# Three edits to a fused attention and two-layer MoE kernel: where tile 2, 3 and 20's softmax and the weight sums run

## The chip, the cores and the metric

One core of a Trainium2 chip runs the whole program. The metric is the device time of one execution in microseconds (us). The kernel before was timed in three runs: 1226.52, 1226.36 and 1223.59 us, median 1226.36 us. The profiled execution took 1226.5 us by the same clock. Its trace covers a span of 1224.7 us, so 1.8 us lie outside the span.

The engines are TensorE (PE; its weight loads are PEld), VectorE (DVE), ScalarE (ACT), GpSimd (POOL) and the sync engine (SP), which issues nearly all DMAs. Each engine works through its own instruction list in order.

## The reference

```
# attention in chunks of 64 rows, 8 heads of 64, 8 batches of 576 rows
scores = q_c @ k_c.T / 8;  attn = exp(scores - max) / (sum + 1e-9);  out = attn @ v_c
x = out as (4608 tokens, 512)
# first layer, w_in 512x2048, w_out 2048x512
h = x @ w_in;  g = h * clip(h + 3, 0, 6) / 6;  x = g @ w_out
# second layer, w_in2 512x1024, w_out2 1024x512
h = x @ w_in2;  solu = h * softmax(h)
y = (solu - mean) / sqrt(var + 1e-6) * g_ln @ w_out2
```

All inputs are float32. Products are done in three passes of a high and a low part: x = hi + lo, x @ w = hi @ w_hi + hi @ w_lo + lo @ w_hi.

## The kernel before, in words

**Tiles and blocks.** The 4608 tokens are 36 tiles of 128 tokens for the attention and 9 blocks of 512 tokens (four tiles) for the first layer. d_ff = 2048 is cut into 16 chunks of 128. The order of all work is the order of the program text (`manual_schedule`): no planner moves anything, an instruction waits only for its data, for its buffer and for the ones before it on its engine.

**The start (L563 to L628).** Tiles 0 to 3 go through attention before any product of the first layer can run. `attn_scores` (L403) takes row maxima on DVE (L398), subtracts them on DVE (L406) and does one exp over the tile on ACT (L410). `attn_norm` (L431) sums rows on DVE (L437), adds 1e-9 (L438), takes the reciprocal (L439) and multiplies (L440), for these four tiles on POOL. `attn_transpose` (L444) turns a tile on PE (L448) and copies it out of PSUM on ACT (L450). `attn_pv` (L465) multiplies by v, casts the high part on ACT (L472); `attn_lo` (L489) subtracts the low part on DVE (L491). Between these, weights are brought from their stored form to hi and lo parts: ACT rescales (L154), DVE takes signs (L163) and words (L171), ACT casts hi (L352), DVE subtracts lo (L358). The second form of softmax, `attn_scores_act` and `attn_exp_act` (L413, L418), does eight exps per tile on ACT, one for each head, straight from PSUM, each with the negative maximum as bias and the row sum as a second output; it is used from tile 4 on. PSUM holds `att` (one buffer), `acc0`, `acc1` and two `hp` buffers.

**Block 0 (L1264).** For each chunk f, PE does hp(f) (12 products, L498), then ACT a Relu (L504), DVE the gate (L513), ACT the cast g_hi (L520), DVE g_lo (L523), and PE adds the chunk before into acc (12 products, L537, `o_next`). DVE and ACT also convert the weights of later chunks in this block. Every fourth chunk has an attention slot for a tile of block 1.

**Blocks 1 and 2 (L1300, F = 0 to 31).** Here the gate writes into PSUM (L508). In every odd F up to 25 there is an attention slot (`att_slot`, L926): scores of one tile and the product with v of another, both into `att`, so the scores of a tile wait until the exps of the one before have read `att`. The exps of a tile run half in one F and half in the next (STEPS, L1287), then comes its norm and 16 transposes of 32x128 on DVE (L460). The weight sums of the seven-product scheme, for j = 0 to 7: `sums_of(j)` at the end of F = 3j on POOL (L993 to L998), then at F = 3j + 1 two casts hi on ACT (L1005) and two subtractions lo on POOL (L1011) with four DMA stores (L1013), through the four `xo` buffers that also take the finished block (L548, L550) on its way to `x2d`.

**The first pair (L1116).** Blocks 3 to 8 go in three pairs, with seven products in place of eight (`mul7`, L1035), for j = 0 to 7: A11, S2, S1, `o_next`, S3, A12, gate and split, `o_next`, `att_slot`, A22, S4. `prep(0)` (L1068) makes the seven operands in eleven steps during F = 21 to 31. Tile 20 (NA) has its scores at F = 25, its softmax in the first form and its norm and transposes (`soft`, `attn_transpose_dve`) inside j = 0 of the pair.

Of the kernel before, what the change touches and what calls it, by code (L numbers as in the profile page):

```python
# [21 lines left out]
def tile_kernel(  # L22
# [394 lines left out]

    def attn_exp_act(u, hs):  # L418
        sc, mx = exps[u]
        if u not in sums:  # L420
            p_t[u] = att_tile(ap2, "p")
            sums[u] = asp.tile([P, H], F32, tag="sm", name="sm")
        for h in hs:
            a, c = h // 2, h % 2
            m = c * NHP + a
            nc.scalar.activation(
                out=p_t[u][:, h], in_=sc[:, c, a], func=AF.Exp, scale=0.125,
                bias=mx[:, m : m + 1], accum_out=sums[u][:, h : h + 1],
            )

    def attn_norm(u, eng=nc.vector):  # L431
        pt = p_t[u]
        if u in sums:
            sm = sums.pop(u)
        else:
            sm = asp.tile([P, H], F32, tag="sm", name="sm")
            nc.vector.tensor_reduce(out=sm, in_=pt, axis=AX.X, op=ALU.add)  # L437
        nc.vector.tensor_scalar_add(out=sm, in0=sm, scalar1=1e-9)  # L438
        nc.vector.reciprocal(out=sm, in_=sm)  # L439
        eng.tensor_mul(  # L440
            out=pt, in0=pt, in1=sm[:, :, None].to_broadcast([P, H, D])
        )

    def attn_transpose(u, pb=None):  # L444
        pt = p_t.pop(u).rearrange("p (a c) k -> p a (c k)", a=NHP)
# [3 lines left out]
        pb = pts[:, u % 2] if pb is None else pb  # L449
        nc.scalar.copy(out=pb, in_=tp.rearrange("p a (e q) -> p (a e) q", e=2))  # L450

# [128 lines left out]
    fetch("o", 1)  # L580
    fetch("i", 3)
    attn_norm(0, nc.gpsimd)
    attn_scores(2, scores(2, att_psum()), qps[0][:, 1])
    attn_norm(1, nc.gpsimd)
    attn_scores(3, scores(3, acc_psum(0)), qps[1][:, 1])
    attn_transpose(0)
    rescale("i", 0)
    attn_norm(2, nc.gpsimd)
    attn_transpose(1)
    attn_pv(0, acc_psum(1), *xs, lo=False)  # L590
    load_v(4)
    fetch("o", 2)
    fetch("i", 4)
    convert(("i", 0))
    attn_norm(3, nc.gpsimd)
    attn_pv(1, att_psum(), *xs, lo=False)
    attn_transpose(2, kbs[0][:, 1])
    load_v(5)
# [4 lines left out]
    attn_lo()  # L603
    split_w(1, nc.vector)
    attn_pv(2, acc_psum(0), *xs, kbs[0][:, 1], lo=False)
    attn_lo()
    rescale("i", 1)
    attn_transpose(3, kbs[1][:, 1])
    attn_lo()
    attn_pv(3, acc_psum(1), *xs, kbs[1][:, 1], lo=False)  # L610
    rescale("o", 0)
    convert_signs(("i", 1))
    attn_lo()
    attn_scores_act(4, scores(4, att_psum()))
    for f in range(5, NF):
# [7 lines left out]
    convert_signs(("o", 0))  # L623
    split_w_lo(nc.vector)
    convert_words()
    rescale("i", 2)
# [359 lines left out]

    def sums_of(j):

        w, s = ([ap1.tile([P, DM], F32, tag=f"tx{i}", name=f"tx{i}") for i in range(2)], None)
        k = slice(0, 2 * P), slice(2 * P, DM)  # L990
        for i in range(2):
            t = wi[2 * j + i].bitcast(F32)
            nc.gpsimd.tensor_add(out=w[i], in0=t[:, 0], in1=t[:, 1])  # L993
# [6 lines left out]

    def split_sums_hi(j):
        s = summed[j]
        hi, lo = ([work_tile("xo", F32R) for _ in range(2)] for _ in range(2))
        for i in range(2):
            nc.scalar.copy(out=hi[i], in_=s[i])  # L1005
        summed[j] = s, hi, lo

    def split_sums_lo(j):
        s, hi, lo = summed.pop(j)
        for i in range(2):  # L1010
            nc.gpsimd.tensor_sub(out=lo[i], in0=s[i], in1=hi[i].bitcast(F32))  # L1011
            for n, t in enumerate((hi[i], lo[i])):
                nc.sync.dma_start(out=sts[j][:, n, i * DM : (i + 1) * DM], in_=t.bitcast(F32))  # L1013

# [99 lines left out]
    h_t2, second = {}, []  # L1114

    def pair(p, todo):  # L1116
        b1, b2 = FIRST + 2 * p, FIRST + 2 * p + 1
# [5 lines left out]
        for j in range(NJ):  # L1123
# [9 lines left out]
            if hang:  # L1133
                t, f = hang
                g = moe_split(t, nc.gpsimd)
                pend.append((b1, f, g))
            while todo:
                todo.pop(0)()
            if u < NU:
                soft(u)  # L1140
# [5 lines left out]
            nc.vector.tensor_add(out=u2, in0=s1, in1=b)  # L1146
            if u < NU:
                attn_transpose_dve(u, range(4))
# [134 lines left out]

    NA = (FIRST + 2) * UPB
    SLOT_AT = {1 + 2 * n: n for n in range(NA - 2 * UPB + 1)}
    PREP_AT = {21: 1, 22: 1, 25: 1, 26: 2, 27: 1, 28: 2, 29: 1, 30: 1, 31: 1}
    STEPS = {}  # L1287
# [12 lines left out]
    for F in range(2 * NF):  # L1300
# [3 lines left out]
        hp, t = moe_h(f, *xn[b])  # L1304
        moe_gate_there(hp, t)
        for step, u, which in STEPS.get(F, []):
            if step == "turn":
# [3 lines left out]
        if F in SLOT_AT:  # L1311
            u = 2 * UPB + SLOT_AT[F]
            att_slot(u - 1 if u > 2 * UPB else None, u + 1 if u + 1 < NA else NA if u == NA else NU)
        o_next()
        for step, u, which in STEPS.get(F, []):
# [5 lines left out]
        if F % 3 == 0 and F // 3 < NJ:  # L1321
            sums_of(F // 3)
        elif F % 3 == 1 and F // 3 < NJ:
            split_sums_hi(F // 3)
            split_sums_lo(F // 3)
        if F < 8:
# [200 lines left out]
```

## Time and profile before

| what | value |
|---|---|
| median of three runs | 1226.36 us (1223.59 to 1226.52) |
| the profiled execution, its span | 1226.5 us, 1224.7 us |
| busy PE, DVE, ACT, POOL | 1190.7, 952.3, 656.9, 381.8 us |
| chain that ended last, PE's share | 83% |
| PE busy in the first 20 us, in the next 20 us | 20 us window: 10.68, 14.81 us |

Busy time is what an engine spends in instructions; the rest of the span it stands idle. The granted clock of TensorE is a share of its full speed: 1.00 is 2.4 GHz, and at 1.2 GHz it is 0.50; a window with 0.91 holds some of each. In a row of the timeline the first number is the start in us from the start of the span, the second the time covered (for xN, from the start of the first to the end of the last), and in brackets stand the idle time of the engine just before and what ended it.

### The profile page before, as it was taken

How to read it: one execution, taken by the hardware profiler on the slowest of the kernel's cores; microseconds unless marked ns; L12 is line 12 of the kernel's file. 1: busy time of each engine (PE TensorE's matmuls, PEld its weight loads, DVE VectorE, ACT ScalarE, POOL GpSimd, SP SyncE). 2: the span in 40 equal slices, each digit the busy share in tenths (PEclk: the TensorE clock that was granted, in tenths of full speed). 3: DMA queues.
4: the chain of work that ended last, by engine and by line, in shares of the span. 5: the costliest groups of instructions: out<-in, count | busy, mean ns of one | idle time of the engine just before them, and what ended most of it. 6: DMA issues, size and time to landing. Idle time of an engine off the chain costs nothing.

```text
span 1224.7 us, 20699 instructions
## 1 busy us (share of the span) xinstructions
PE 1190.7 (97%) x7268; PEld 970.7 (79%) x7268; DVE 952.3 (78%) x1754; ACT 656.9 (54%) x1353; POOL 381.8 (31%) x466
## 2 busy tenths in 40 slices
PE   6899999999999999999999999999989999999998
PEld 5677788878788888888888888887768888888887
DVE  7999687787677779777778777774997878878774
ACT  4676455453322237322246343363788777877775
POOL 3000243530011110011100112100676767665865
PEclk9999999999999999999999999999999999999999
DMA  9800584441355537355445798794222323232311
GB/s 369 362 26 27 210 304 132 159 152 61 104 198 207 194 108 249 108 189 190 175 138 201 264 335 291 252 377 174 86 68 90 99 71 99 72 97 69 100 54 63
DMA packets 110360, 199.82 MB, mean 163 GB/s; under 512 B 14000, under 2 KB 49072, under 8 KB 107184
## 3 DMA queue, kind: packets, MB, share of 16 engines
q1 hardware_dynamic: 103920, 186.97, 44.1%
q10 hardware_dynamic: 6336, 11.54, 2.5%
q8 instruction: 57, 0.93, 0.3%
q14 instruction: 47, 0.39, 0.1%
HBM read 129.50 MB, written 58.20 MB: 153 GB/s over the span
## 4 chain that ended last, share of the span: by engine, by line
PE 83%; DVE 11%; ACT 2%; issue 1%; DMA 1%; SPq 1%; POOL 1%; DVEq 0%; ACTq 0%; POOLq 0%
PE acc L537 28%; PE po L882 14%; PE hp L1040 14%; PE hp L498 7%; PE att L1040 5%; PE b L684 5%; PE c L684 3%; PE a L684 3%; PE att L386 3%; DVE s L171 2%; DVE g_lo L523 1%; SPq L797 1%; DVE s L163 1%; DVE pbd L460 1%; PE att L684 1%
## 5 line engine op out<-in xcount | busy, mean ns | idle before, releaser
L537 PE MATMUL acc<-g_hi,wo 128*128 128x512 f32 x1152 | 294.9, 393 | 1.4 <-ACT g_hi L520 1.3
L537 PEld LDWEIGHTS acc<-g_hi,wo 128*128 128x128 f32 x1152 | 215.4, 189 | 48.8 <-DVE xo L550 1.9
L523 POOL TENSOR_TENSOR g_lo<-t,g_hi 128x512 fp32r<-128x512 f32 x45 | 65.6, 1457 | 450.8 <-ACT g_hi L520 450.8
L537 PE MATMUL acc<-g_lo,wo 128*128 128x512 f32 x576 | 160.0, 389 | 1.3 <-DVE g_lo L523 1.3
L882 PE MATMUL po<-wi,wo 128*128 128x512 f32 x648 | 152.5, 392 | 1.3 <-ACT ob L891 1.3
L882 PEld LDWEIGHTS po<-wi,wo 128*128 128x128 f32 x648 | 122.6, 189 | 27.5 <-ACT ob L891 1.7
L1040 PE MATMUL hp<-wi,ws 128*128 128x512 f32 x576 | 142.7, 390 | 0.0
L460 DVE STREAM_TRANSPOSE pbd<-p 32x128 f32<-32x128 f32 x448 | 135.5, 303 | 6.7
L537 PEld LDWEIGHTS acc<-g_lo,wo 128*128 128x128 f32 x576 | 108.2, 188 | 24.3 <-DVE g_lo L523 1.7
L1040 PEld LDWEIGHTS hp<-wi,ws 128*128 128x128 f32 x576 | 107.9, 188 | 23.7 <-DVE s L1146 1.2
L665 POOL TENSOR_TENSOR x_lo<-xr,x_hi 128x768 fp32r<-128x768 f32 (+1 forms) x32 | 70.3, 2218 | 135.0 <-DVE xr L651 64.0
L797 ACT COPY wo<-wo 32x256 f32<-32x256 f32 x228 | 92.0, 404 | 17.4 <-DVE wo L779 11.3
L498 PE MATMUL hp<-x_hi,wi 128*128 128x512 f32 x384 | 97.9, 397 | 2.0 <-ACT wi L352 1.9
L520 ACT CAST g_hi<-t 128x512 fp32r<-128x512 f32 x112 | 69.4, 620 | 53.0 <-DVE t L513 36.0
L498 PEld LDWEIGHTS hp<-x_hi,wi 128*128 128x128 f32 x384 | 72.5, 191 | 18.9 <-ACT wi L352 2.7
L1106 ACT ACTIVATE t<-att,three 128x512 f32<-128x512 f32 x24 | 16.5, 688 | 130.4 <-PE att L1040 113.8
L769 DVE SCALAR_TENSOR_TENSOR wo<-wo,r,wo 128x1024 f32<-128x1024 f32 x36 | 77.4, 2151 | 1.3
L1011 POOL TENSOR_TENSOR xo<-tx,xo 128x512 fp32r<-128x512 f32 x16 | 20.8, 1320 | 181.7 <-ACT xo L1005 167.0
L1040 PE MATMUL att<-wi,wa 128*128 128x512 f32 x288 | 73.1, 389 | 0.0
L866 POOL TENSOR_TENSOR wo<-wo,wo 128x1024 fp32r<-128x1024 f32 x26 | 63.4, 2439 | 6.8 <-ACT wo L862 3.3
L1040 PEld LDWEIGHTS att<-wi,wa 128*128 128x128 f32 x288 | 54.1, 188 | 11.3
L504 ACT ACTIVATE t<-hp,three 128x512 f32<-128x512 f32 x48 | 33.1, 691 | 50.4 <-PE hp L498 50.4
(269 smaller groups left out, 2194.6 us busy)
## 6 DMA issues: line engine op xcount, KB each, us to landing
ws<-sts SPq DMA_DIRECT2D x24, 1024.0 KB, 6.7
wa<-stw SPq DMA_DIRECT2D x24, 512.0 KB, 4.0
held<-xo SPq DMA_DIRECT2D x42, 256.0 KB, 2.2
s<-held SPq DMA_DIRECT2D x42, 256.0 KB, 4.4
wo<-wo SPq DMA_DIRECT2D x328, 32.0 KB, 1.8
x2d<-xo SPq DMA_DIRECT2D x36, 256.0 KB, 3.0
out<-ob SPq DMA_DIRECT2D x36, 256.0 KB, 2.2
v<-in_v SPq DMA_DIRECT2D x34, 256.0 KB, 2.7
```

The lines of the kernel that those rows point to most:

```text
L460: nc.vector.transpose(out=pb[o : o + 32, s // 2, s % 2], in_=pv[s * 32 : s * 32 + 32, c, e],)
L498: nc.tensor.matmul(hp, wi[f][:, a, kk * P : (kk + 1) * P], b[:, kk], start=(n == 0), stop=(n == 3 * KD - 1),)
L520: nc.scalar.copy(out=g_hi, in_=t)
L523: eng.tensor_sub(out=g_lo, in0=t, in1=g_hi.bitcast(F32))
L537: nc.tensor.matmul(acc[dc], wo[f][:, w, dc * P : (dc + 1) * P], g[i], start=(at == 0 and n == 0), stop=(at == NF - 1 and n == 2),)
L665: eng.tensor_sub(out=lo[:, f], in0=r, in1=hi[:, f].bitcast(F32))
L684: nc.tensor.matmul(ps, x[:, AT[a], j], w2[w, j][i], start=(start and n == 0), stop=(stop and n == 5), skip_group_check=True,)
L769: nc.vector.scalar_tensor_tensor(out=h, in0=e, scalar=r, in1=h, op0=ALU.mult, op1=ALU.mult, accum_out=mu)
L797: move(out=m[b * 32 : b * 32 + 32, a], in_=tr[a * 32 : a * 32 + 32, b])
L866: eng.tensor_sub(out=lo, in0=m, in1=hi.bitcast(F32))
L882: nc.tensor.matmul(po, a[f], wi[KD * NS + f][:, w], start=(n == 0), stop=(n == 3 * NF2 - 1),)
L1040: nc.tensor.matmul(ps, w[:, i, kk * P : (kk + 1) * P], x[:, kk], start=(start and n == 0), stop=(stop and n == 5), skip_group_check=True,)
```

## The change

Three edits, and two small moves that go with them.

1. Start: tiles 2 and 3 take the second form of softmax, their norm's multiplication moves from POOL to DVE, the copies after the PE transposes of tiles 1 and 3 move from ACT to DVE, and the steps stand in another order. Tile 4's maxima come later. The row sums `sm` get four buffers.
2. Weight sums: `split_sums(j, i)` does one cast, one subtraction and two stores; it runs once per chunk, at F = 3j + 2 and 3j + 3, between the Relu and the cast of g, instead of twice at the end of F = 3j + 1. `sums_of(0)` gets a one-column copy on POOL in front, which reads the low part g[1] of F = 0; for j > 0 there is none (`None if F else g[1]`).
3. Tile 20: its norm runs at the end of F = 27, its transposes at F = 28 and 29, and not inside j = 0 of the first pair. `prep` runs one step later from F = 27 on, its eleventh step (B22) in j = 0 of the pair after the sum u2. The `o_next` of F = 31 is left out there, so two chunks are pending when the pair begins.

```
-    def attn_exp_act(u, hs):
+    def attn_exp_act(u, hs, pt=None):
...
-            sums[u] = asp.tile([P, H], F32, tag="sm", name="sm")
+            sums[u] = asp.tile([P, H], F32, tag="sm", name="sm", bufs=4)
...
-    def attn_transpose(u, pb=None):
+    def attn_transpose(u, pb=None, copy=nc.scalar.copy):
...
-        nc.scalar.copy(out=pb, in_=tp.rearrange("p a (e q) -> p (a e) q", e=2))
+        copy(out=pb, in_=tp.rearrange("p a (e q) -> p (a e) q", e=2))
...
+    attn_scores_act(2, scores(2, att_psum()))
     attn_norm(0, nc.gpsimd)
-    attn_scores(2, scores(2, att_psum()), qps[0][:, 1])
+    attn_scores_act(3, scores(3, acc_psum(0)))
     attn_norm(1, nc.gpsimd)
-    attn_scores(3, scores(3, acc_psum(0)), qps[1][:, 1])
+    attn_exp_act(2, range(H), qps[0][:, 1])
+    rescale("i", 0)
+    attn_exp_act(3, range(H // 2), qps[1][:, 1])
     attn_transpose(0)
-    rescale("i", 0)
-    attn_norm(2, nc.gpsimd)
-    attn_transpose(1)
+    attn_exp_act(3, range(H // 2, H))
+    attn_norm(2)
+    convert_signs(("i", 0))
+    attn_transpose(1, copy=nc.vector.tensor_copy)
+    convert_words()
     attn_pv(0, acc_psum(1), *xs, lo=False)
...
-    convert(("i", 0))
-    attn_norm(3, nc.gpsimd)
+    attn_norm(3)
+    split_w_hi()
+    attn_transpose(2, kbs[0][:, 1])
     attn_pv(1, att_psum(), *xs, lo=False)
-    attn_transpose(2, kbs[0][:, 1])
...
     attn_lo()
-    split_w(1, nc.vector)
+    attn_transpose(3, kbs[1][:, 1], copy=nc.vector.tensor_copy)
+    split_w_lo(nc.vector)
     attn_pv(2, acc_psum(0), *xs, kbs[0][:, 1], lo=False)
     attn_lo()
     rescale("i", 1)
-    attn_transpose(3, kbs[1][:, 1])
+    attn_pv(3, acc_psum(1), *xs, kbs[1][:, 1], lo=False)
     attn_lo()
-    attn_pv(3, acc_psum(1), *xs, kbs[1][:, 1], lo=False)
...
-    attn_scores_act(4, scores(4, att_psum()))
+    sc = scores(4, att_psum())
...
     split_w_lo(nc.vector)
+    attn_scores_act(4, sc)
     convert_words()
...
+        if after is not None:
+            nc.gpsimd.tensor_copy(out=w[0][:, :1], in_=after[:, :1].bitcast(F32))
...
-    def split_sums_hi(j):
...
-    def split_sums_lo(j):
...
+    def split_sums(j, i):
+        w = summed[j][i]
+        hi, lo = (work_tile("xo", F32R) for _ in range(2))
+        nc.scalar.copy(out=hi, in_=w)
+        nc.gpsimd.tensor_sub(out=lo, in0=w, in1=hi.bitcast(F32))
+        for n, t in enumerate((hi, lo)):
+            nc.sync.dma_start(out=sts[j][:, n, i * DM : (i + 1) * DM], in_=t.bitcast(F32))
...
-            while todo:
+            for _ in todo[:-1]:
                 todo.pop(0)()
-            if u < NU:
+            if u < NU and u != NA:
                 soft(u)
...
             nc.vector.tensor_add(out=u2, in0=s1, in1=b)
-            if u < NU:
+            while todo:
+                todo.pop(0)()
+            if u < NU and u != NA:
                 attn_transpose_dve(u, range(4))
...
-    PREP_AT = {21: 1, 22: 1, 25: 1, 26: 2, 27: 1, 28: 2, 29: 1, 30: 1, 31: 1}
+    PREP_AT = {21: 1, 22: 1, 25: 1, 26: 2, 28: 1, 29: 1, 30: 1, 31: 2}
...
         moe_gate_there(hp, t)
+        if (F - 2) // 3 in summed and F % 3 != 1:
+            split_sums((F - 2) // 3, 1 - (F - 2) % 3)
...
-        o_next()
+        if F < 2 * NF - 1:
+            o_next()
...
-            sums_of(F // 3)
-        elif F % 3 == 1 and F // 3 < NJ:
-            split_sums_hi(F // 3)
-            split_sums_lo(F // 3)
+            sums_of(F // 3, None if F else g[1])
+        if F == 27:
+            soft(NA)
+        elif F in (28, 29):
+            attn_transpose_dve(NA, range(2 * F - 56, 2 * F - 54))
```

## Rows read from the trace of the kernel before

**Rows 1.** The page, busy time of each engine and its share of the span
```profile
PE 1190.7 (97%) x7268; PEld 970.7 (79%) x7268; DVE 952.3 (78%) x1754; ACT 656.9 (54%) x1353; POOL 381.8 (31%) x466
```

**Rows 2.** Waits of PE: waiting for whom, us in total, times, longest
```profile
PE att L386 <- ACT p L426: 5.5, 3, 2.8
```

**Rows 3.** Windows of 20 us: busy us (instructions) by engine, granted clock, DMA
```profile
140.00:160.00 20.00, 17.72 (x151) 14.20 (x154) 13.71 (x33) 11.25 (x44) 9.14 (x9) 1.00 0.69 259
...
240.00:260.00 20.00, 17.18 (x127) 13.83 (x127) 16.82 (x45) 10.19 (x43) 11.37 (x11) 0.91 0.73 247
...
320.00:340.00 20.00, 17.45 (x130) 14.29 (x129) 14.94 (x33) 6.70 (x13) 1.27 (x1) 0.91 0.57 190
```

**Rows 4.** Windows by groups of four chunks of block 0 (PE, PEld, DVE, ACT, POOL)
```profile
22.90:45.00 22.10, 17.54 (x69) 12.26 (x62) 21.38 (x36) 13.26 (x35) 5.34 (x5) 0.89 1.03 416
45.00:69.90 24.90, 24.49 (x169) 19.65 (x169) 24.80 (x48) 17.40 (x43) 0.00 (x0) 1.00 0.51 205
69.90:94.30 24.40, 24.01 (x166) 19.32 (x165) 24.30 (x47) 17.39 (x43) 0.00 (x0) 1.00 0.11 33
94.30:117.90 23.60, 23.60 (x166) 19.41 (x165) 23.46 (x45) 16.92 (x41) 0.00 (x0) 1.00 0.11 35
```

**Rows 5.** Lines of the weight conversion on DVE: ns min/median/max, first and last start
```profile
L171 DVE SCALAR_TENSOR_TENSOR s<-wo,s x32: 679/683/1666, 27.1 to 119.3; 128x512 int32<-128x512 int32 x32
...
L163 DVE TENSOR_SCALAR s<-wo x16: 415/420/968, 25.6 to 117.7; 128x512 int32<-128x512 int32 x16
...
L358 DVE TENSOR_TENSOR wo<-s,wo x16: 679/684/1201, 30.2 to 122.3; 128x512 fp32r<-128x512 f32 x16
```

**Rows 6.** Timeline of the start, 0 to 45 us
```profile
8.80 0.68 DVE L437 TENSOR_REDUCE sm<-p 128x8 f32<-128x512 f32 x1
...
10.07 1.04 POOL L440 TENSOR_TENSOR p<-p,sm 128x512 f32<-128x512 f32 x1 [8.73 <-DVE sm L439]
...
14.08 0.57 ACT L450 COPY pbd<-hp 128x512 f32<-128x512 f32 x1
...
22.89 0.69 DVE L491 TENSOR_TENSOR x_lo<-acc,x_hi 128x512 fp32r<-128x512 f32 x1 [1.02 <-ACT x_hi L472]
...
29.36 0.68 DVE L513 SCALAR_TENSOR_TENSOR t<-t,hp 128x512 f32<-128x512 f32 x1
...
30.60 0.31 ACT L426 ACTIVATE p<-att,mx 128x64 f32<-128x64 f32 x1
...
37.26 3.77 PE L498 MATMUL hp<-x_hi,wi 128*128 128x512 f32 x8 [1.92 <-ACT wi L352]
```

**Rows 7.** Timeline of blocks 1 and 2, at F = 1 and at F = 16
```profile
137.10 0.70 DVE L508 SCALAR_TENSOR_TENSOR hp<-t,hp 128x512 f32<-128x512 f32 x1
...
143.15 1.15 ACT L1005 CAST xo<-tx 128x512 fp32r<-128x512 f32 x2
...
236.16 0.62 ACT L1005 CAST xo<-tx 128x512 fp32r<-128x512 f32 x1 [2.46 <-DMA x2d<-xo]
```

**Rows 8.** Norm on DVE (ns min/median/max), and weight sums on POOL (busy us, mean ns)
```profile
L438 DVE TENSOR_SCALAR sm<-sm x36: 155/170/734, 9.5 to 614.3; 128x8 f32<-128x8 f32 x36
...
L440 DVE TENSOR_TENSOR p<-p,sm x32: 691/692/1424, 44.1 to 614.7; 128x512 f32<-128x512 f32 x32
...
L993 POOL TENSOR_TENSOR tx<-wi 128x512 f32<-128x512 f32 x16 | 20.7, 1317 | 6.3 <-DVE wi L358 6.3
```

**Rows 9.** Timeline from F = 31 into j = 0 of the first pair
```profile
319.88 1.98 PE L537 MATMUL acc<-g_hi,wo 128*128 128x512 f32 x8
...
322.21 0.69 DVE L523 TENSOR_TENSOR g_lo<-hp,g_hi 128x512 fp32r<-128x512 f32 x1 [0.65 <-ACT g_hi L520]
...
326.38 5.04 DVE L460 STREAM_TRANSPOSE pbd<-p 32x128 f32<-32x128 f32 x16
...
331.46 1.29 DVE L550 TENSOR_SCALAR xo<-acc 128x512 f32<-128x512 f32 x2
...
334.83 1.13 PE L386 MATMUL att<-kbd,q 64*64 64x64 f32 x32 [2.56 <-DVE t L513]
```

More of the change, by code (lines that the diff above doesn't have):

```diff
@@ L416, in attn_scores_act @@
         exps[u] = sc, mx
-    def attn_exp_act(u, hs):
+    def attn_exp_act(u, hs, pt=None):
         sc, mx = exps[u]
         if u not in sums:
-            p_t[u] = att_tile(ap2, "p")
-            sums[u] = asp.tile([P, H], F32, tag="sm", name="sm")
+            p_t[u] = att_tile(ap2, "p") if pt is None else pt
+            sums[u] = asp.tile([P, H], F32, tag="sm", name="sm", bufs=4)
         for h in hs:
@@ L435, in attn_norm @@
         else:
-            sm = asp.tile([P, H], F32, tag="sm", name="sm")
+            sm = asp.tile([P, H], F32, tag="sm", name="sm", bufs=4)
             nc.vector.tensor_reduce(out=sm, in_=pt, axis=AX.X, op=ALU.add)
@@ L985, in tile_kernel, with sums_of @@
     ORDER = ("S2", "S4", "S3", "S1")
-    def sums_of(j):
+    def sums_of(j, after=None):
         w, s = ([ap1.tile([P, DM], F32, tag=f"tx{i}", name=f"tx{i}") for i in range(2)], None)
         k = slice(0, 2 * P), slice(2 * P, DM)
+        if after is not None:
+            nc.gpsimd.tensor_copy(out=w[0][:, :1], in_=after[:, :1].bitcast(F32))
         for i in range(2):
@@ L999, in sums_of @@
         summed[j] = w
-    def split_sums_hi(j):
[L1002 to L1006, printed above, removed]
-    def split_sums_lo(j):
[L1009 to L1013, printed above, removed]
+    def split_sums(j, i):
[5 more added lines that the diff above has]
+            nc.sync.dma_start(out=sts[j][:, n, i * DM : (i + 1) * DM], in_=t.bitcast(F32))
     NJ = NF // 2
@@ L1114, in tile_kernel @@
     h_t2, second = {}, []
+    NA = (FIRST + 2) * UPB
     def pair(p, todo):
@@ L1282, in tile_kernel @@
         rescale("i", f + 4)
-    NA = (FIRST + 2) * UPB
     SLOT_AT = {1 + 2 * n: n for n in range(NA - 2 * UPB + 1)}
-    PREP_AT = {21: 1, 22: 1, 25: 1, 26: 2, 27: 1, 28: 2, 29: 1, 30: 1, 31: 1}
+    PREP_AT = {21: 1, 22: 1, 25: 1, 26: 2, 28: 1, 29: 1, 30: 1, 31: 2}
     STEPS = {}
```

## The prediction

> **What bounds the kernel now.** I read the busy times first: PE is busy 1190.7 of 1224.7 us [rows 1], and the change removes no product. So it can only win back PE idle time, 34 us in all, and time at the lower clock. The 20 us windows show where that is outside the start and the tail: beyond 100 us most windows have PE at 20.00, and three do not [rows 3]. 140 to 160 lacks 2.28 us at full clock; 240 to 260 lacks 2.82 us and has a granted clock of 0.91; 320 to 340 lacks 2.55 us, also at 0.91. A mean of 0.91 over 20 us means 3.6 us at 1.2 GHz in place of 2.4 GHz, in which 0.09 x 20 = 1.8 us of work are lost. So the second and third stall cost 4.6 and 4.35 us, the first 2.28.
>
> The waits say who ends them: scores into `att` waiting for the exps of the tile before, three times and 5.5 us together [rows 2], which holds the first two stalls, and once the gate of chunk j = 0 [rows 9].
>
> The start and block 0 are the other place. There DVE, not PE, is full: 21.38 of 22.10, 24.80 of 24.90 and 24.30 of 24.40 us [rows 4]. A group of four chunks takes 24.4 us while DVE is full and 23.6 where PE alone decides. So whatever brings DVE forward before 45 us brings the end of block 0 forward by the same amount.
>
> **Part 1, the start.** DVE loses two subtractions and two row sums of 0.68 us, 2.7 us together [rows 6]. It gains two 128x8 multiplications of 0.17, two norm multiplications of 0.69 [rows 8] and two copies out of PSUM; the trace has such a copy only on ACT, 0.57 us [rows 6], and I take 0.69 as for DVE's other 128x512 work. Sum +3.1. So the amount of work stays within 0.4 us. The waits change: now DVE stands idle 1.02 us before the third low part, at 22.89 [rows 6], because tile 3's norm on POOL (1.04 us) [rows 6], PE's turn and ACT's cast lie in its way. In the new order the chain is: both maxima and row sums 0 and 1 done at about 13.45; POOL's second norm to 14.65; PE's turn of tile 1 (about 1.1 us) to 15.8; then DVE without a gap but one of some 0.4 us: copy, words, norm 3, low part 0, copy 3, low part of w, low parts 1 and 2, signs, low part 3. Back to back these start 0.6 us apart for the big ones, 7.4 us together, and end at 23.3 against 23.58 now. ACT gets 16 exps of 0.31 [rows 6] and loses two exps and two copies, about +2 us; they run from 10.4 to 16.5, before the casts they could delay. I take -0.3. Bounds: -1.5 if both waits vanish, +1.5 if DVE's two copies each wait for a turn of PE.
>
> The larger effect comes from a line in another edit. `sums_of(0)` now runs on POOL between 20 and 33 us, while DVE converts weights. The conversion lines show it: one L171 takes 1.666 against a median of 0.683, one L163 0.968 against 0.420 and its neighbour on wi the same, one L358 1.201 against 0.684 [rows 5]; the later instances, with POOL idle [rows 4], stay at the median. Together 0.98 + 0.55 + 0.55 + 0.52 = 2.6 us, all before 33 us and on DVE's full chain: the gate of chunk 0 at 29.36 and PE's hp of chunk 2 at 37.26 [rows 6] stand behind them. With the copy that reads g[1] of F = 0, POOL starts these sums at about 130.6, so the 2.6 us go. Next late is PE itself, which has 0.4 us of stall left per group. Part 1 with this: **-2.9 us** (bounds -4.5 to +1.5, the upper one if PE's slower stretch at 37 us, x8 in 3.77 us [rows 6], or a DMA sets the pace and not DVE).
>
> **Part 2, the weight sums.** At F = 16, four `xo` buffers hold the finished block 1 on its way to DRAM, and ACT's second cast waits 2.46 us for one of them [rows 7]. Behind it in ACT's queue stand the Relu of F = 17, its g cast and the exps of tile 17. Everything after is late by about 4 us, and at F = 19 the scores wait. In the new order no cast stands in F = 16 (16 = 3 x 5 + 1). The one at F = 17 takes the first of the four buffers, free some 3 us before the second one, just when the Relu is done; the second pair of buffers is asked for 5.4 us later. Only POOL's subtraction waits (to 236.2), and the SP queue behind it, which delays the loads of v, q and k to about 238; they are needed at 245. So the stall goes: -4.6. Otherwise ACT pays nothing for a cast between Relu and g cast: it has to wait there for the gate, 0.70 us, and the cast takes 0.62 [rows 7].
>
> At F = 1, two casts (1.15 us [rows 7], 1.03 to the next start) stand between tile 9's first exps and the Relu of F = 2, on the chain that ends in the stall of 2.28. They go: -1.03. But POOL's first sums now lie at 130.6 to 137, beside tile 8's norm, which delays the gate of F = 1 to 137.10 [rows 7]. L438 and L440 have been as long as 0.734 and 1.424 against 0.170 and 0.692 [rows 8]: up to 1.3 us more. I take +0.35, since by the clock of the two engines the norm's multiplication meets the end of one short POOL sum. Net **-0.7** (bounds -1.03 to +0.3).
>
> Here the Trainium skill speaks against the change: SBUF — State Buffer, section "Who interferes with whom", says that a DVE instruction with two SBUF inputs, or in a two-port mode, and a GpSimd instruction that reads SBUF block each other for the whole instruction, whoever starts first. By that rule each of the two could wait for a whole sum of 1.32 us (L993) [rows 8], 2.6 us in place of 1.3, and the part would end at +1.6, 2.3 later than I take it; the longest instances in the trace bear the blocking out and not that length.
>
> **Part 3, the pair's start.** In j = 0 DVE has, between u2 and u3, 16 transposes of 5.04 us and two `xo` copies of 1.29 [rows 9], and before them tile 20's norm, 1.74 us. So the gate of A12 comes late: PE has finished A12 at 332.3 and waits 2.56 us, to 334.83 [rows 9]. Moved out are 6.8 us of DVE; B22's step comes in with 1.28. Then the gate is done about 1.6 us after A12's end, and meanwhile PE has the second pending `o_next`, 2.72 us, which the left-out one of F = 31 supplies. So PE does not stand still: -4.35. Cover that is gone: without that product at 319.88, A11 and S2 (1.36 each) lead to S1 at 322.6, and its buffer is that of hp(31), free when g_lo ends at 322.9 [rows 9]: +0.35. T4's step now lies in F = 31 and delays s1 and so u2 to about 326.5, while S3 starts at 327: no cost, but a margin of 0.5. In F = 27 to 29 DVE takes the 6.8 us in three chunks of 5.44, each then 5.2 to 5.9 full; g is needed some 3 us later than it is ready, so nothing waits. Net **-4.0** (bounds -4.35 to -1.5, if S3 waits for u2 and the clock falls all the same).
>
> **Sum.** -2.9 - 4.6 - 0.7 - 4.0 = -12.2 from the profiled 1226.5: 1214.3 us. That execution stands 0.1 above the median, so the same holds for it.
>
> **Rivals.**
> (a) The start gives nothing or loses: DVE waits for PE's turns, and the 2.6 us turn into waits for ACT's casts or the weights. For it: two DVE copies now stand behind PE, and DMA is full until 45 us [rows 4]. Against: the rescales on ACT show no wait for a DMA. Then -9.3 to -8: 1217 to 1218.5.
> (b) One of the two big stalls stays, because the exps or the gate are late by another way (POOL beside DVE at F = 18; u2 late in the pair). For it: DVE is at 16.82 of 20 us in that window [rows 3]. It gives 4.6 less: about 1219.
> (c) PE's slower stretch at 37 us goes too, because the stalls ahead of it shrink: 1.8 more, about 1212.
> (d) Slower: the cast of a weight sum stands in front of the g cast in 16 chunks, so ACT blocks there whenever POOL's sum or an `xo` buffer is late, as at F = 16 now. Each such place costs up to 4.6 us; with three new ones the gain of 12.2 is gone, and one more gives 1232. For it: POOL's sums and subtraction take some 8 us per j beside DVE. Against: two chunks (10.9 us) lie between a sum and its first cast.
> (e) The copy on POOL does not hold the sums back, and they run at 20 us as now: 2.6 less, 1217.
> (f) At F = 0 the sums hold both steps of tile 8's norm for a whole POOL instruction each, 1.32 us [rows 8], and the stall at F = 3 grows: 2.3 us less gain, 1216.6. For it: the longest L440 lost 0.73. Against: the median norm stays at its shortest, 0.69, though POOL works through half of these blocks. This is what the page of the Trainium skill named above would make of it.
>
> **How the numbers follow.** Forecast 0.52, own range 1212 to 1216.5; (a) with (e) 0.19; (f) 0.06; (b) 0.11; (c) 0.07; (d) 0.05. From 1211 to 1219.5 holds the forecast, (a), (e), (f), (c) and most of (b). A measurement of this kernel can tell 0.3%, 3.7 us, from no change; so 1222.7 is the border of faster. All but (d) and two stalls staying at once lie below: faster 0.92, same 0.05, slower 0.03.
>
> **What would show it.** Windows at 140, 240 and 320 us: PE at about 18.4 in the first and 20 in the others, clock 1.00 in the last two. L171, L163 and L358 without an instance above 1 us before 40 us; the first L993 at about 128. Hp of chunk 2 some 3 us before 37.26. In the pair, scores directly behind the second `o_next`. The prediction is wrong if hp of chunk 2 starts later than 36, or if PE waits for ACT at F = 19.

## The result, and the profile after

The changed kernel takes 1214.88 us (median of six runs, 1213.93 to 1216.41); the kernel before took 1226.44 us beside it (six runs, 1223.59 to 1228.46). The ratio is 0.9909, with a 95% interval of 0.9894 to 0.9923. Its profiled execution took 1215.1 us (span 1213.3), 11.4 less than that of before. Some lines stand lower in the file now: the weight sums' L993 of before is L1001, the casts' L1005 is L1012, the subtractions' L1011 is L1013, the operand step's L1057 is L1059.

PE does the same 7268 products in 4.2 us less busy time than in [rows 1]; the other 7.2 us of the shorter span are idle time that went.

```profile
PE 1186.5 (98%) x7268; PEld 967.4 (80%) x7268; DVE 952.9 (79%) x1756; ACT 659.5 (54%) x1381; POOL 379.3 (31%) x465
```

The waits of PE between 100 and 360 us (engine and line, whom it waited for, us in total, times, longest). Where [rows 2] has 5.5 us for ACT there are 2.0, two small waits are new, and the 2.56 us ahead of the pair's scores [rows 9] are gone.

```profile
PE att L386 <- ACT p L426: 2.0, 3, 1.4
PE att L386 <- DVE pbd L460: 0.3, 1, 0.3
PE hp L1042 <- DVE g_lo L523: 0.2, 1, 0.2
```

The windows that answer to [rows 3], in the same columns. The second and third, which lacked 2.8 and 2.6 us at a clock of 0.91, are full at 1.00. The first still lacks 1.4 us, and 260 to 280, which was not on my list, lacks 0.57.

```profile
140.00:160.00 20.00, 18.62 (x200) 15.07 (x199) 15.72 (x36) 11.32 (x40) 9.69 (x9) 1.00 0.76 278
240.00:260.00 20.00, 20.00 (x206) 16.29 (x205) 15.88 (x39) 10.96 (x40) 10.21 (x11) 1.00 0.64 210
260.00:280.00 20.00, 19.43 (x171) 15.59 (x170) 16.97 (x42) 8.57 (x23) 4.64 (x5) 1.00 0.22 79
...
320.00:340.00 20.00, 20.00 (x148) 16.42 (x147) 15.70 (x34) 6.35 (x12) 2.90 (x2) 1.00 0.61 217
```

The conversions on DVE, against [rows 5]: the longest is as long as the median. In the first group of block 0 POOL is idle, where [rows 4] had 5.34 us of it, and DVE is as full as before.

```profile
L171 DVE SCALAR_TENSOR_TENSOR s<-wo,s x32: 683/689/697, 26.1 to 115.8; 128x512 int32<-128x512 int32 x32
L163 DVE TENSOR_SCALAR s<-wo x16: 418/422/428, 23.9 to 114.2; 128x512 int32<-128x512 int32 x16
L358 DVE TENSOR_TENSOR wo<-s,wo x16: 683/685/694, 28.3 to 118.7; 128x512 fp32r<-128x512 f32 x16
```

```profile
22.90:45.00 22.10, 18.62 (x77) 13.78 (x75) 21.38 (x42) 15.50 (x39) 0.00 (x0) 0.92 1.03 416
```

To say where the 11.4 us come from, I take the start of the same PE product in both profiles at seven places, and the difference after minus before:

| place | before | after | difference | since the place above |
|---|---|---|---|---|
| scores in slot F = 1 (all of start and block 0) | 133.41 | 129.89 | -3.52 | -3.52 |
| scores in slot F = 3 | 147.49 | 143.10 | -4.39 | -0.87 |
| scores in slot F = 17 | 232.9 | 228.5 | -4.41 | 0.0 |
| scores in slot F = 21, after the stall of F = 19 | 262.1 | 252.9 | -9.17 | -4.76 |
| scores in slot F = 25 | 286.0 | 277.9 | -8.10 | +1.07 |
| scores in j = 1 of the first pair | 352.6 | 340.9 | -11.68 | -3.58 |
| last product (its end) | 1220.9 | 1209.5 | -11.40 | +0.28 |

Against the predicted -2.9, -0.7, -4.6, 0 and -4.0, each of the steps forecast has its place and nearly its size; the +1.07 between F = 21 and F = 25 was not forecast.

The start, against [rows 6]: the last of the four low parts, tile 3's (22.89 before), has no idle time ahead of it, the gate (29.36) is 1.92 us earlier, and hp of chunk 2 (37.26) 3.53 us earlier. The 1.89 us that PE waits for ACT there are as long as before. Two instructions of DVE ahead of it are long beside POOL's norms: L415 takes 0.63 us, where its other instance there takes 0.17, and the first L440 1.42, where the second takes 0.69. Behind hp's first four products the next four take 1.94 us (last row), so PE's slower stretch of [rows 6] is still there.

```profile
11.35 0.63 DVE L415 TENSOR_SCALAR mx<-mx 128x8 f32<-128x8 f32 x1
...
13.32 1.42 DVE L440 TENSOR_TENSOR wo<-wo,sm 128x512 f32<-128x512 f32 x1
...
21.95 0.68 DVE L491 TENSOR_TENSOR x_lo<-acc,x_hi 128x512 fp32r<-128x512 f32 x1
...
27.44 0.68 DVE L513 SCALAR_TENSOR_TENSOR t<-t,hp 128x512 f32<-128x512 f32 x1
...
33.73 1.19 PE L498 MATMUL hp<-x_hi,wi 128*128 128x512 f32 x4 [1.89 <-ACT wi L352]
...
35.43 1.94 PE L498 MATMUL hp<-x_hi,wi 128*128 128x512 f32 x4 [0.51 <-DVE wi L358]
```

The first weight sums, and the casts of j = 5 that answer to [rows 7]. POOL's copy and first sum start at 127, and tile 8's norm multiplication (L440), which meets the third, shorter sum, takes 0.86 in place of 0.69. The two casts, of which the second waited 2.46 us at 236.16, now stand at F = 17 (229.21) and F = 18 (235.96), each directly behind the Relu. It is POOL's subtraction for the first of them that waits, 6.98 us for `x2d`, and no wait of PE follows from it.

```profile
127.00 0.18 POOL L998 COPY tx<-g_lo 128x1 f32<-128x1 f32 x1 [112.80 <-ACT xo L548]
127.27 2.53 POOL L1001 TENSOR_TENSOR tx<-wi 128x512 f32<-128x512 f32 x2
129.88 0.75 POOL L1003 TENSOR_TENSOR tx<-tx 128x256 f32<-128x256 f32 x1
...
130.31 0.86 DVE L440 TENSOR_TENSOR p<-p,sm 128x512 f32<-128x512 f32 x1
...
228.62 0.69 ACT L504 ACTIVATE t<-hp,three 128x512 f32<-128x512 f32 x1 [0.33 <-PE hp L498]
229.21 0.61 ACT L1012 CAST xo<-tx 128x512 fp32r<-128x512 f32 x1
...
232.24 1.29 POOL L1013 TENSOR_TENSOR xo<-tx,xo 128x512 fp32r<-128x512 f32 x1 [6.98 <-DMA x2d<-xo]
...
235.38 0.69 ACT L504 ACTIVATE t<-hp,three 128x512 f32<-128x512 f32 x1 [0.49 <-PE hp L498]
235.96 0.61 ACT L1012 CAST xo<-tx 128x512 fp32r<-128x512 f32 x1
```

The pair, against [rows 9]: S1 waits 0.20 us for its buffer, and the scores start directly behind the second `o_next`, where they waited 2.56 us.

```profile
314.86 1.67 PE L1042 MATMUL hp<-wi,ws 128*128 128x512 f32 x6 [0.20 <-DVE g_lo L523]
...
323.64 1.07 PE L537 MATMUL acc<-g_lo,wo 128*128 128x512 f32 x4
324.64 0.69 PE L386 MATMUL att<-kbd,q 64*64 64x64 f32 x32
```

The new stall lies at F = 23. In before POOL's sums for j = 7 ran ahead of the slot of F = 21, whose scores start at 262.1:

```profile
256.62 2.55 POOL L993 TENSOR_TENSOR tx<-wi 128x512 f32<-128x512 f32 x2
```

After, these scores start at 252.9 and the sums only at 255.73, behind the second subtraction of j = 6, which waits 4.15 us for its cast at F = 21. DVE's small multiplication (L415, 0.17 without POOL), the norm multiplication (0.69) and the operand step of F = 21 (L1059, 1.22 in before) now lie beside them and take 0.56, 1.43 and 1.54 us. Together these three are 1.45 us longer. The gate behind them starts at 262.87, 9.96 us behind the scores of F = 21, where before has 8.52 (270.60), and PE waits twice near 265.5.

```profile
254.35 1.30 POOL L1013 TENSOR_TENSOR xo<-tx,xo 128x512 fp32r<-128x512 f32 x1 [4.15 <-ACT xo L1012]
255.73 2.54 POOL L1001 TENSOR_TENSOR tx<-wi 128x512 f32<-128x512 f32 x2
...
256.49 0.56 DVE L415 TENSOR_SCALAR mx<-mx 128x8 f32<-128x8 f32 x1
257.39 1.43 DVE L440 TENSOR_TENSOR p<-p,sm 128x512 f32<-128x512 f32 x1
261.41 1.54 DVE L1059 TENSOR_TENSOR wi<-xr,wi 128x1024 fp32r<-128x1024 f32 x1
262.87 0.68 DVE L508 SCALAR_TENSOR_TENSOR hp<-t,hp 128x512 f32<-128x512 f32 x1
...
265.42 0.43 PE L386 MATMUL att<-pbd,v 64*64 64x64 f32 x6 [0.25 <-ACT p L426]
266.18 0.68 PE L386 MATMUL att<-pbd,v 64*64 64x64 f32 x26 [0.33 <-DVE pbd L460]
```

### The profile page after: what moved, and what is told of

It reads as the page before. It is cut to its first block, busy times and chain, and to the rows that moved or that the text cites. A ratio compares the mean times of both kernels' runs of the same rounds, so it can differ in the third digit from the quotient of the medians.

```text
span 1213.3 us, 20739 instructions
## 1 busy us (share of the span) xinstructions
PE 1186.5 (98%) x7268; PEld 967.4 (80%) x7268; DVE 952.9 (79%) x1756; ACT 659.5 (54%) x1381; POOL 379.3 (31%) x465
## 4 chain that ended last, share of the span: by engine, by line
PE 84%; DVE 11%; ACT 2%; issue 1%; SPq 1%; DMA 1%; POOL 1%; DVEq 0%; ACTq 0%; POOLq 0%
PE acc L537 29%; PE po L888 14%; PE hp L1042 14%; PE hp L498 7%; PE att L1042 5%; PE b L690 5%; PE c L690 3%; PE a L690 3%; PE att L386 3%; DVE s L171 2%; DVE g_lo L523 1%; DVE pbd L460 1%; DVE wo L775 1%; DVE s L163 1%; PE att L690 1%
## 5 line engine op out<-in xcount | busy, mean ns | idle before, releaser
L803 ACT COPY wo<-wo 32x256 f32<-32x256 f32 x228 | 92.0, 404 | 17.5 <-DVE wo L785 11.4
L523 DVE TENSOR_TENSOR g_lo<-t,g_hi 128x512 fp32r<-128x512 f32 x67 | 46.2, 690 | 14.7 <-PE acc L537 12.5
```

The lines of the kernel that those rows point to most:

```text
L523: eng.tensor_sub(out=g_lo, in0=t, in1=g_hi.bitcast(F32))
L803: move(out=m[b * 32 : b * 32 + 32, a], in_=tr[a * 32 : a * 32 + 32, b])
```

## Experiments: the parts alone

The theory is the prediction's: four gains in four places, which add up. Each part alone, made from the kernel before, tells whether it has its own place.

**The order of the start alone** (`e1_start`): the first edit; the copy ahead of `sums_of(0)`, which the prediction counts with the start, is not in it.

```
+    attn_scores_act(2, scores(2, att_psum()))
...
-    attn_norm(2, nc.gpsimd)
+    attn_norm(2)
...
+    attn_transpose(3, kbs[1][:, 1], copy=nc.vector.tensor_copy)
...
```

> Kernel before with the new order of the start alone (tiles 2 and 3 on ScalarE, their norm on VectorE, two copies on VectorE, four sum buffers); the weight sums and the pair as before. Theory: the order alone brings VectorE's last low part of the start forward by what the trace after shows, 22.89 to 21.95, and the sums of chunk 0 still run on GpSimd before 33 us and still stretch VectorE's conversions by some 2.6 us. So hp of chunk 2 starts near 36.3, and the time is 0.9 us below before (0.3 to 1.5). Rival: the order gives the whole 3.5 us seen at the start, and the sums beside it cost nothing: hp of chunk 2 at 33.7, 3.5 us below before.

Measured: 1224.19 against 1226.43 us, ratio 0.9981 (0.9968 to 0.9993). In the profile the scores of F = 1 start at 133.31, 0.10 before those of before. Hp of chunk 2 starts at 37.19, where 36.3 was expected and before has 37.26. The sums still run at the start, and long conversions stay, though the longest is 1.10 us and not 1.67:

```profile
L171 DVE SCALAR_TENSOR_TENSOR s<-wo,s x32: 672/681/1104, 28.1 to 119.2; 128x512 int32<-128x512 int32 x32
```

Of the 2.0 us that this profile is shorter at its last product, 1.6 come in the last 350 us, where the clock fell in before and not here (last section). The median is 2.2 us lower, outside the expected 0.3 to 1.5, and this part of the profile is the likely reason. The order is worth little of the start's 3.5 us, as the theory had it.

**The copy alone** (`e2_gate`).

```
...
-            sums_of(F // 3)
+            sums_of(F // 3, None if F else g[1])
```

> Kernel before with nothing but the one-column copy in front of the first weight sums, which reads the low part of g of F = 0. Theory: GpSimd's first sums move from 20 to 33 us to behind 130 us, no L171, L163 or L358 is longer than 0.75 us after 21 us, hp of chunk 2 starts 2.6 us earlier (34.6), and the time falls by 2.3 us: 2.6 less some 0.3 that the norm at F = 0 loses to the sums, which stand beside it now. Rival: VectorE's chain is not what sets block 0's pace, and the time stays within 0.5 us. Second rival: the sums at F = 0 cost two full GpSimd instructions, and the gain is 0.3 us or less.

Measured: 1222.10 against 1226.43 us, ratio 0.9967 (0.9955 to 0.9979). The scores of F = 1 start at 130.32, 3.09 earlier, and hp of chunk 2 at 34.19. That is more than the 2.6 expected there, and 0.4 to 0.5 us of it is chance: the scores of tile 3 start at 9.16 here and at 9.59 in before, before anything in them differs. From F = 1 to F = 3 it costs 0.16 more, where 0.3 was expected. The median is 4.3 us lower and not 2.3; in the profiles 1.6 us of that lie behind j = 1, where the clock fell in before and not here. One column of POOL's copy, 0.18 us, carries the larger part of the start.

**The split per chunk alone** (`e3_sums`), without the copy.

```
...
+        if (F - 2) // 3 in summed and F % 3 != 1:
+            split_sums((F - 2) // 3, 1 - (F - 2) % 3)
...
-        elif F % 3 == 1 and F // 3 < NJ:
-            split_sums_hi(F // 3)
-            split_sums_lo(F // 3)
```

> Kernel before with the casts of the weight sums one per chunk, between Relu and the cast of g; no copy in front of the first sums, start and pair as before. Theory: the stall at F = 19 goes with its time at the lower clock (4.7 us), the one at F = 3 falls from 2.28 to about 1.25 (1.0 us), and the new stall at F = 23, which costs 1.1 us in the changed kernel, comes in: 4.6 us below before. Rival: the stall at F = 23 comes from tile 20's move or from the shift of the operands' steps, and not from the sums: then 5.7 us below before.

Measured: 1222.26 against 1226.43 us, ratio 0.9964 (0.9952 to 0.9976). From F = 1 to F = 3 it gains 1.04 us, from F = 17 to F = 21 4.8 us, and then it loses 1.07 with the same new wait as the changed kernel; the 2.6 us at j = 0 are still there. The waits of PE between 100 and 360 us:

```profile
PE att L386 <- DVE t L513: 2.6, 1, 2.6
PE att L386 <- ACT p L426: 1.8, 3, 1.2
PE att L386 <- DVE pbd L460: 0.3, 1, 0.3
```

So the new stall at F = 23 belongs to the split, not to tile 20.

**Tile 20 alone** (`e4_tile20`): the third edit, with `prep` and the left-out `o_next`.

```
...
-    PREP_AT = {21: 1, 22: 1, 25: 1, 26: 2, 27: 1, 28: 2, 29: 1, 30: 1, 31: 1}
+    PREP_AT = {21: 1, 22: 1, 25: 1, 26: 2, 28: 1, 29: 1, 30: 1, 31: 2}
...
-        o_next()
+        if F < 2 * NF - 1:
+            o_next()
...
+        if F == 27:
+            soft(NA)
+        elif F in (28, 29):
+            attn_transpose_dve(NA, range(2 * F - 56, 2 * F - 54))
```

> Kernel before with part 3 alone: tile 20's norm and transposes at F = 27 to 29, the operands' steps one later, the products of the next-to-last chunk carried into the pair. Theory: the stall of 2.56 us at j = 0 and its time at the lower clock (1.8) go, and 0.5 us come in where S1 waits for its buffer: 3.6 us below before. Rival: with the stall gone the next pair's loads come too late and part of it is given back: less than 2 us below before.

Measured: 1224.43 against 1226.43 us, ratio 0.9980 (0.9971 to 0.9990). Between F = 25 and j = 1 the profile gains 3.63 us on that of before, the changed kernel 3.58. The medians move 2.0 us only, not the 3.6 expected. One reason is in the profiles: before's is one of those in which the clock fell at j = 0, and it does not always fall there (last section). The rival's reason, later loads, does not show: from j = 1 to the last product this profile takes 868.4 us and before 868.3. Against the profile's gain stand its start, 0.8 us later by chance, and 1.5 us of lower clock behind F = 3, where the clock did not fall in before.

## Experiments: inside the parts

**The change without the copy** (`e5_no_gate`).

```
-            sums_of(F // 3, None if F else g[1])
+            sums_of(F // 3)
```

> The changed kernel without the one-column copy in front of the first weight sums. Theory: GpSimd's first sums return to some 20 to 33 us and stretch VectorE's conversions again by 2 to 2.6 us; the part at F = 3 gains back 0.1 to 0.3. Time 1217.0 (1216.2 to 1218.5). Rival: in the new order VectorE's chain has slack at this place, and the time stays at 1214.9 within 0.5 us.

Measured: 1216.52 against 1226.20 us, ratio 0.9924 (0.9910 to 0.9937), 1.6 above the changed kernel's own median and inside the expected range; the two intervals overlap, so the profile has to carry the reading. Its scores of F = 1 start at 132.70, and the long conversions are back:

```profile
L171 DVE SCALAR_TENSOR_TENSOR s<-wo,s x32: 674/682/1103, 27.5 to 118.6; 128x512 int32<-128x512 int32 x32
...
L358 DVE TENSOR_TENSOR wo<-s,wo x16: 678/684/1198, 30.0 to 121.6; 128x512 fp32r<-128x512 f32 x16
```

**Only the left-out product** (`e6_onext`), and **only tile 20's softmax** (`e7_soft20`).

```
-        o_next()
+        if F < 2 * NF - 1:
+            o_next()
```

> Kernel before with only the products of the next-to-last chunk carried into the pair; tile 20's norm and transposes still inside j = 0, the operands' steps as before. Theory: the transposes still make the gate late (near 333.5 on the clock of before), but 12 products lie between A12 and the scores, so PE waits about 1.0 us there in place of 2.56 and some 0.3 us at S1; the clock does not fall. Time 1.3 us below before where the clock does not fall in either, up to 3 where it fell before. Rival: the late gate alone decides, and PE still waits 2 us or more before the scores of tile 21.

```
-            if u < NU:
+            if u < NU and u != NA:
                 soft(u)
...
+        if F == 27:
+            soft(NA)
...
```

> Kernel before with only tile 20's norm and transposes moved to F = 27 to 29; every product and operand step where it was. Theory: the gate of j = 0 is now bound by Relu and gate alone behind A12, about 1.5 us after its end, and no product lies in between: PE waits 1.5 us in place of 2.56. Time 1.0 us below before, up to 2.8 where the clock fell before. So each half takes away less than the whole stall, and both together leave none. Rival: with VectorE free the stall goes whole: 2.5 us or more below before.

Measured: 1224.76 and 1224.48 against 1226.20 us, ratios 0.9982 (0.9972 to 0.9992) and 0.9989 (0.9978 to 1.0000). The second is not clear of noise, so the reading rests on the waits. The wait before the scores of j = 0 shrinks from 2.56 to 0.7 with the one (first row) and to 1.5 with the other (second row), and with both it is gone: the product that covers and the work that moves out each close a part. In both profiles the clock stayed at 1.00 there.

```profile
PE att L386 <- DVE t L513: 0.7, 1, 0.7
```

```profile
PE att L386 <- DVE t L513: 1.5, 1, 1.5
```

**One pair of casts, one chunk later** (`e8_j5`), to tell the four-buffer theory of the F = 19 stall from one in which all sixteen casts matter.

```
-        elif F % 3 == 1 and F // 3 < NJ:
+        elif F == 17 or F % 3 == 1 and F // 3 < NJ and F != 16:
```

> Kernel before with one thing changed: the two casts of the weight sums of j = 5 stand at the end of F = 17 and not of F = 16, where the xo buffers hold the finished block 1. Theory: ScalarE's wait of 2.46 us for a DMA is what makes F = 17 and 18 late; PE no longer waits at F = 19 (2.82 us before) and keeps its clock there: 3 to 4.7 us below before, nearly all that the new place of all sixteen casts gives at F = 19. Rival: the cast's own 1.15 us and GpSimd beside VectorE make F = 19 late, and a stall of at least 1.5 us stays: less than 2.5 us below before.

Measured: 1222.16 against 1226.20 us, ratio 0.9969 (0.9957 to 0.9982). From F = 17 to F = 21 it gains 4.76 us, the same as all sixteen moved casts, and the 240 us window (here 25 us wide) is full:

```profile
240.00:265.00 25.00, 25.00 (x228) 20.45 (x227) 19.33 (x52) 13.59 (x50) 15.85 (x16) 1.00 0.71 233
```

It has no stall at F = 23 either. So the whole gain at F = 19 comes from two casts that no longer ask for `xo` buffers while block 1 leaves through them.

**What is left: the two remaining stalls** (`v1_prep`, `v2_late`, and both, `v3_both`), from the changed kernel. The text for the first names F = 23 where the list had F = 22: the steps of F = 21 and 22 go to 22 and 24.

```
-    PREP_AT = {21: 1, 22: 1, 25: 1, 26: 2, 28: 1, 29: 1, 30: 1, 31: 2}
+    PREP_AT = {22: 1, 24: 1, 25: 1, 26: 2, 28: 1, 29: 1, 30: 1, 31: 2}
```

> The changed kernel with the operand steps of the first chunk's two middle buffers (B11, B21) one slot later, at F=22 and F=24 instead of F=21 and F=23. Theory: in the changed kernel sums_of(7) on POOL (255.73 to 261.9 us) lies beside the operand step of F=21, whose DVE conversions of 0.56 and 1.43 us hold the gate of F=22 until 262.87 and PE twice (0.25 and 0.33 us) near 265.4: 1.07 us over before between F=21 and F=25. One slot later the step finds POOL done: no wait of PE before F=23 and 1.0 us less than the changed kernel, 1213.9 us. Rival: the two short waits come from the sums themselves (late weights or a late g), not from the operand step: the waits stay and the time is the changed kernel's, 1214.9 within 0.4. Second rival: the step at F=22 and F=24 is late for its own slot or lies beside the next sums, and the stall moves by a slot: 1214.9 to 1216.

Measured: 1213.31 against 1225.68 us, ratio 0.9900 (0.9885 to 0.9915). By the intervals none of these three can be told from the changed kernel (0.9894 to 0.9923); what they show is read from the stretches of their profiles. L415 and L440 still take 0.56 and 1.43 beside the sums, but the gate of F = 22 now follows the first transposes with no operand step in between, PE waits nowhere near it, and the step itself (last row) takes 1.22 in place of 1.54, with POOL done. F = 21 to F = 25 costs 0.00 more than before, in place of +1.07.

```profile
260.01 2.53 DVE L460 STREAM_TRANSPOSE pbd<-p 32x128 f32<-32x128 f32 x8
262.58 0.70 DVE L508 SCALAR_TENSOR_TENSOR hp<-t,hp 128x512 f32<-128x512 f32 x1
...
266.49 1.22 DVE L1059 TENSOR_TENSOR wi<-xr,wi 128x1024 fp32r<-128x1024 f32 x1
```

The second moves tile 8's sixteen transposes behind the maxima of tile 9.

```
-    STEPS.setdefault(0, []).extend([("exp", u, range(H)), ("norm", u, (0, 1))])
-    STEPS.setdefault(1, []).append(("turn", u, (2, 3)))
+    STEPS.setdefault(0, []).extend([("exp", u, range(H)), ("norm", u, ())])
+    STEPS.setdefault(1, []).append(("late", u, range(4)))
...
+            elif step == "late":
+                attn_transpose_dve(u, which)
```

> The changed kernel with tile 8's sixteen transposes behind the second weight sum's scores at the end of F=1 instead of ahead of them. Theory: the 1.38 us that PE still waits at F=3 in the changed kernel is for tile 8's scores' exponentials, which are held up because the transposes with their evictions lie between; later they fill that time: stall gone, 1.4 us less, 1213.5 us. Rival: the wait is for ScalarE's casts and not for the order on PE: the wait stays and the transposes' 1 to 1.5 us lie behind it as before, 1214.9 us; or the later evictions hold the scores of tile 8 and the wait grows by as much, 1216 us.

Measured: 1213.89 against 1225.68 us, ratio 0.9904 (0.9887 to 0.9920). Tile 9's first exps start at 134.28 in place of 138.62, and PE does not wait at F = 3:

```profile
134.28 0.31 ACT L426 ACTIVATE p<-att,mx 128x64 f32<-128x64 f32 x1 [1.62 <-DVE mx L415]
...
141.87 0.69 PE L386 MATMUL att<-kbd,q 64*64 64x64 f32 x32
```

From F = 1 to F = 3 this is 2.35 us less than before, 1.48 less than the changed kernel. The reason that I wrote for it named the order of tile 8's exps on PE; the rows show another: eight transposes (2.5 us) stood on DVE ahead of the gate of F = 1 and eight behind it, and tile 9's maxima, for which ACT's exps wait, came after both.

> The changed kernel with both: operand steps B11 and B21 at F=22 and F=24, and tile 8's transposes at the end of F=1. Theory: the two gains lie in different slots and add up, 1.0 + 1.4 us less than the changed kernel, 1212.5 us. Rival: one of the two gives nothing (see the kernels alone), 1213.5 to 1214; or PE without either gap is at the throttled clock longer in the sixteen steps and gives a part back, 1213.5.

Measured: 1212.49 against 1225.68 us, ratio 0.9893 (0.9878 to 0.9907), the lowest median of all. In its profile the two gains stand side by side (F = 1 to F = 3 2.35 us less than before, F = 21 to F = 25 0.00). Between 100 and 360 us PE waits 0.6 us in all, 0.4 for ACT at F = 1 and the 0.20 of S1.

## Why the prediction was right, step by step

The forecast of 1214.3 lies 0.6 below the median.

**The start, predicted -2.9, measured -3.5.** The two profiles differ by chance there as well: tile 2's scores, which wait for their load in both, start at 8.32 in before and at 7.62 after, and these 0.7 us are as large as the miss. The six profiles with the old start (before, and the third, fourth, sixth, seventh and eighth experiment) have the scores of F = 1 at 133.20 to 134.21, mean 133.8; the two with the new order but without the copy at 133.31 and 132.70, mean 133.0; the four with both (after and the last three) at 129.89 to 131.03, mean 130.4; the one with the copy but the old order at 130.32. So the copy gives 2.6 in the new order, which is its term, and 3.5 in the old one; the order gives 0.8 without the copy and nothing beside it. Profiles of one start lie up to 1 us apart, so these runs don't settle the order's term (-0.3), and its bounds hold either. Its working had two costs too little: beside POOL's norms DVE's L415 took 0.63 and not 0.17, and its first norm multiplication 1.42 and not 0.69. Rival (a) and rival (e) fall with the copy's 2.6 us. Rival (c) did not come: the slower stretch of PE is still there in the changed kernel (four products in 1.94 us at 35.43). In the second experiment it is gone (the same four take 1.19 us, granted clock 1.00), and the scores of F = 1 are no earlier for it.

**F = 3, predicted -0.7, measured -0.87.** The casts that moved away gave 1.04 (third experiment), where 1.03 was taken. Rival (f), that the norm is held for two whole sums, fell: L440 took 0.17 more, half of the 0.35 that I took, and L438 stayed at 0.17. The reason is the time at which they meet, as forecast: the sums start at 127.27, on the clock of before 130.8 for the forecast 130.6, so the two long ones are over at 129.80, L438 starts at 129.87 and L440 meets only the end of one of 0.75 us. The margin was 0.07 us. At F = 21 the same meeting falls out otherwise. There L440 takes 1.43 beside one sum, the length the longest instance of [rows 8] had shown, and L415 and L1059 are held too. The rule of the Trainium skill (SBUF — State Buffer, "Who interferes with whom": an instruction of DVE with two SBUF inputs, or in a two-port mode, and one of GpSimd that reads SBUF block each other for the whole instruction) agrees with these rows: the holds here are 0.17 to 0.74 us, each about the rest of the POOL instruction that was running. Where DVE starts just behind POOL the hold is nearly the whole of it: L415 at 146.93 takes 1.23 in place of 0.17 beside a sum of 1.27, and outside the places of this change L657 at 862.24 takes 2.62 in place of 0.42 beside a POOL instruction of 2.46 that began 0.13 us earlier. So rival (f) fell by the time at which the norm came, not because such a hold can't be that long.

**F = 19, predicted -4.6, measured -4.76.** Stall and fall of the clock both went, for the reason given (eighth experiment). POOL's subtraction waits to 232.24, which is 236.65 on the clock of before; 236.2 was forecast.

**F = 21 to F = 25, predicted 0, measured +1.07.** Here the prediction failed, by leaving a step out. I followed what waits on ACT behind each cast, but on POOL only one waiting subtraction and its SP queue. The second subtraction of j = 6, now at F = 21, stands in POOL's queue ahead of `sums_of(7)` and waits there for ACT's cast, so the sums start 2.8 us behind the scores of F = 21 and not 5.5 us ahead of them. The split alone shows the same loss, the kernel in which the casts stayed in pairs does not, and moving the operand step takes it back (third, eighth and ninth experiment). Rival (b) named the kind of place (POOL beside DVE), but at F = 18 and at 4.6 us.

**The pair, predicted -4.0, measured -3.58.** The fall of the clock (1.49, for which I had 1.8) went, and so did the stall: A12 starts 4.07 us ahead of the scores before, 2.71 more than its own 1.36. S1 starts 0.36 us late by the pace of the six products ahead of it, 0.35 as predicted, 0.20 of it in the waits. Another 0.26 us, which I had not counted, lie in the starts behind it, 0.14 of them in S1 itself (1.50 in place of 1.36). The margin of S3 held. That the clock's fall was there to be won is in part luck: the forecast took it as certain, and at j = 0 it came in three of five profiles (last section).

**Rival (d)** did not come up: ACT's waits in F = 0 to 31 are for PE and DVE, the longest 4.2 us, none is for an `xo` buffer, and the one long wait for `xo` (6.98) is POOL's.

The four gains came in their places, and three for the reasons given; at the start the copy's reason held and the order's share stays open. That the sum came out within 1 us is luck in part: the errors, -0.6 at the start, -0.2 at F = 3, -0.2 at F = 19, +1.1 at F = 23, +0.4 in the pair and +0.3 behind it, cancel down to the 0.8 us by which the profiled 1215.1 stands above 1214.3.

## What to carry to other kernels

A stall of the busiest engine is worth following to the buffer whose release ends it: at F = 19 that was a store of another block through a shared ring, and two casts, one chunk later, gave all of 4.8 us in the profiles. Work on GpSimd that nobody waits for isn't free while VectorE is full: holding it back by a one-column copy gave some 2.6 us at the start, and letting it slip beside another slot cost 1.1. So where an instruction is moved into a queue in which it will wait, follow the instructions behind it to their new neighbours, the ones that were not moved included.

## What the runs showed of the hardware

The same stall of PE does not always bring the clock down. After the stall at F = 3 (2.2 to 2.4 us) the granted clock stayed at 1.00 in before (first row) and in the sixth experiment, and fell to the lower level (1.2 GHz) for a while in five other profiles with that stall, as in the first experiment (second row), where F = 3 to F = 5 takes 1.5 us longer.

```profile
140.00:165.00 25.00, 22.72 (x217) 18.44 (x217) 17.34 (x41) 13.82 (x53) 13.99 (x14) 1.00 0.73 272
```

```profile
140.00:165.00 25.00, 22.76 (x211) 18.55 (x210) 15.72 (x36) 12.98 (x46) 13.14 (x13) 0.93 0.69 258
```

After the 2.56 us of j = 0 it fell in before, in the third and in the eighth experiment, and not in the first and second; from j = 0 to j = 1 the scores then lie 17.8 us apart and not 16.3. After the 2.5 to 3.0 us at F = 19 it fell in all six profiles that have this stall; from F = 19 to F = 21 these take 13.7 to 14.1 us, and 12.2 where the stall is gone. A wait of 2.0 us near 905 us, which no version touches, brought it down in the changed kernel (first row: after) and not in the last version (second row), and that is most of the 1.6 us by which their stretches behind 861 us differ.

```profile
900.00:920.00 20.00, 17.81 (x71) 13.91 (x70) 16.06 (x25) 15.95 (x30) 14.93 (x21) 0.91 0.32 98
```

```profile
900.00:920.00 20.00, 17.84 (x78) 14.31 (x78) 18.20 (x29) 15.52 (x29) 15.77 (x19) 1.00 0.32 98
```

So a stall of 2 to 3 us had two prices here, its own idle time for certain and some 1.5 to 1.9 us of lower clock in a part of the profiles. What decides it was not tried.
